# Query tensor of the first two batches spread over 128 partitions, score products in four row tiles, and a new order for the opening of a memory-attention and feed-forward kernel

## Chip, core and metric

The kernel runs on one core of a Trainium2 chip. The metric is the device time of one execution in microseconds (us). Before the change three runs took 653.88, 654.03 and 655.69 us, so the median is 654.03 us.

## What is computed

For each of 8 batches and 8 heads there are 576 positions, a head size of 64 and 32 memory slots. A softmax over the positions turns `phi` into weights, these gather `k` and `v` into 32 slots, and the queries attend to the slots. The result goes through a two-layer feed-forward stage.

```python
a = softmax(phi, axis=2)                        # over the 576 positions
k_m = einsum('bhsm,bhsd->bhmd', a, k)
v_m = einsum('bhsm,bhsd->bhmd', a, v)
attn = softmax(q @ k_m.T / sqrt(64), axis=-1)   # over the 32 slots
x = (attn @ v_m)  ->  (4608, 512)
h = x @ w_in                                    # 512 x 2048, 64-bit floats in memory
out = maximum(0.01 * h, h) @ w_out              # 2048 x 512, 64-bit floats in memory
```

## The kernel before

**Staging.** The slot values `v_m` are multiplied into `w_in` ahead of time (the "fold", `fold_products`, L1003), so that the first layer is a product of the attention weights with a folded weight, and the second layer a product with `w_out`. The 4608 rows are worked through in groups. Group 0 (384 rows of batch 0) is computed in f32 straight from the weights, since the split of the weights into pairs of f16 words is not there yet; all later groups use three f16 products for one. The opening is the part from the first instruction to the end of group 0. In it the first two batches' attention, the loading of the weights and their conversion from 64-bit floats, and group 0 itself run beside each other.

**Names.** Each step has a name in a dictionary, and two strings of names, `OPENING` (L47) and `LATER` (L67), give the order in which the steps are written. Each engine takes its instructions in exactly that order. The steps that the change and the prediction speak of:

- `a0.phi0`, `a0.k`, `a0.q0`, `a0.v`: loads of batch 0, issued on SyncE's queue (SP). `i0.ld0` to `i0.ld2` load the first quarter of `w_in` in three pieces (768, 768 and 512 columns), `o0.ld0` to `o0.ld2` that of `w_out`. A staging tile of eight slots (`ld_slot`) takes q and the pieces in turn.
- `a0.A10`, `a0.A11` (L592): maxima of phi on DVE. `a0.A2` (L633) transposes them on PE, `a0.A3` (L640, L643) reduces them and writes a diagonal matrix, `a0.B0` (L649) spreads them to all partitions with a product of ones by that diagonal. `B1x` subtracts (L658), `B2x` is the exponential on ACT (L664), `B3` sums (L680 to L683).
- `a0.C10`, `a0.C11` (L698): 72 small products each that gather k and v into slots. `C2` (L712) transposes the sums, `C30` (L721 to L726) turns them into factors, `C3k` (L743, ACT) scales the slots of k and lays them out three times side by side, `C31` (L754, DVE) scales those of v into `x_v`. `C4` (L762, L337, L339) and `D2` (L344) find the largest slot value.
- `D10` (L777): four PE transposes of the scaled k into 96 partitions, `D3` (L799) copies them to `kT`. `Q0`, `Q1` (L845): DVE transposes of q in blocks of 32. `E10`, `E1` (L887): score products, 24 each for batch 0, in three row tiles of 32 by four column tiles of 32. `E20` to `E22` (L908): DVE transposes of the scores.
- `S01` to `S06`: the softmax of the first two thirds of batch 0 (maximum L928, subtract L931, exponential L936, sum L940 to L942, scale L945, transpose L953). `S11` to `S18`: the last third.
- `D11` (L785) and `D5` (L805): the transpose of `x_v` into `vT`. `f00.1` (L1020): the first fold, eight products of 64 by 32 by 512. `f00.2` (L1370): its copy into `w_mem`. `f01`, `f02`, `f03` are the other quarters.
- `i0.y0` (L397, ACT), `i0.h0` (L386 on ACT or L388 on DVE), `i0.t0` (L406, DVE): the two halves of a 64-bit word are scaled or shifted and put together as one f32 word, for piece 0 of the first quarter of `w_in`; `i0.b` (L411) sums squares.
- `u0.P0` (L1114): the first product of group 0, two f32 products of 128 x 384. `u0.V0` (L1121) is its activation, `u0.O0` (L1186) three f32 products of 128 x 512 with `w_out`. There are 16 of each.
- `z.1`, `z.3`, `z.4` (L1387): that many products of a tile of ones, whose result nobody reads.

A product of f32 operands appears in the trace as two MATMUL records.

q of batches 0 and 1 is loaded to 96 partitions, six positions to a partition:

```python
t = (ld_slot() if b < FB else at(IO * g, IO))[:CP].rearrange(
    "p (hh j d) -> p hh j d", hh=HP, j=NJ
)
nc.sync.dma_start(
    t, q[b].rearrange("(hh g) (p j) d -> g p hh j d", g=NG, j=NJ)[g]
)
```

k, v and phi are already loaded to 128 partitions, nine positions to a partition.

Of the kernel before, what the change touches and what calls it, by code (L numbers as in the profile page):

```python
# [40 lines left out]
a0.C10 i0.ld0 i0.ld1 a0.B3 a0.C2 i0.ld2 z.1 a0.C30 a0.v a0.C3k a0.D10 a0.Q0 a0.D3 a0.E10 a0.Q1
a0.E1 i0.y0 i0.h0 o0.ld0 i0.t0 z.3 a0.E21 a0.E20 i0.y1 i0.h1 o0.ld2 a0.S01 o0.ld1 o1.ld0 i0.y2
i0.h2 i0.t2 a0.C11 a0.S02 i0.t1 a0.S03 i0.b a0.E22 a0.S11 a0.C31 o0.y0 a0.D11 a0.S12 a0.D5 f00.1
o0.h0 a0.S04 i1.ld1 o0.y2 a0.S05 f00.2 a0.S06 a0.C4 z.1 a0.S13 u0.P0 a0.D2 o0.t0 a0.S14 a0.S15
a0.D4 i1.ld0 o0.h1 u0.V0 o0.y1 u1.P0 u1.P1 o0.h2 u1.V0 o0.t2 i1.ld2 a0.S16 o1.ld2 o1.y0 o1.h0 u0.O0
# [5 lines left out]
i2.b u4.V0 a1.B20 u5.P0 a1.B3 o0.b a1.C10 i3.ld2 a1.Q0 i3.ld1 a1.C2 u5.V0 o1.b u2.O1 i3.y0 u5.P1
u4.V1 a1.C30 a1.C31 a1.C3k a1.C4 a1.D10 a1.D2 o2.b i3.h0 a1.D3 a1.Q1 i3.y2 i3.h2 a1.D11 a1.D4 u3.O1
i3.t2 a1.E1 o3.ld0 a1.D5 i3.y1 u4.O0 i3.h1 i3.t0 o3.h0 u5.V1 o3.y0 o3.ld2 u5.O0 a1.E20 i3.t1 a1.E21
i3.b ci.1 o3.ld1 a1.E22 f03.1 a1.S01 a1.S11 a1.S02 a1.S03 a1.S04 u4.O1 o3.y2 o3.y1 o3.h2 ci.2 o3.t0
f03.2 a1.S12 ci.3 ci.4 e. o3.h1 o3.t1 a1.S05 u6.P0 u6.V0 a1.S13 a1.S06 a1.S07 u6.P1 u7.P0 a1.S14
a1.S15 o3.t2 w0.2 u7.V0 u6.O0 a1.S16 o3.b w1.1 co.1 co.2 u7.O0 w1.2 co.3 u6.V1 co.4 u5.O1 o0.k0
# [1423 lines left out]
```

## Time and profile before

| | |
|---|---|
| median of three runs (lowest, highest) | 654.03 us (653.88, 655.69) |
| profiled execution: from its first to its last instruction (span) | 653.4 us |
| what lies around that span (lowest run less the span) | 0.5 us |
| PE busy | 635.2 us, 97% of the span |
| DVE busy | 515.4 us, 79% |
| ACT busy | 392.5 us, 60% |
| mean granted PE clock | 0.995 |
| moved by DMA | 61.16 MB |

For the profiled execution the profile gives no other time than its span. The page of the profile gives busy times of an engine, then digits for 40 equal slices of the span (16.3 us each), then groups of instructions. An engine's timeline lists instructions in order of time: start, duration, engine, line, operation, output and input, count, and in brackets the idle time ahead of it with what ended it. A row of the view by stretches gives, for each stretch, the busy time and number of instructions of PE, weight loads, DVE, ACT and GpSimd, then the granted PE clock, the busy share of the DMA engines and the GB/s that they moved.

### The profile page before, as it was taken

The numbers are of one execution on the slowest core, as the hardware profiler recorded it, in microseconds if no ns is written. First come the engines' busy times: TensorE is split into PE (matmuls) and PEld (weight loads), VectorE is DVE, ScalarE is ACT, GpSimd is POOL, SyncE is SP. The second block draws the span as 40 slices with busy tenths as digits, with TensorE's granted clock in tenths as the row PEclk, the third lists the DMA queues.
The fourth block names the chain that finished last, engine by engine and source line by source line (L and its number), as shares of the span: only waits on it lengthen the run. The fifth ranks groups of instructions, "written<-read, shape, count | busy, mean of one in ns | idle before, by whom it ended". The sixth has DMA issues, their size and how long they took to land.

```text
span 653.4 us, 17090 instructions
## 1 busy us (share of the span) xinstructions
PE 635.2 (97%) x7256; PEld 476.3 (73%) x7256; DVE 515.4 (79%) x863; ACT 392.5 (60%) x671; POOL 29.5 (5%) x37
## 2 busy tenths in 40 slices
PE   6799999999999999999999999999999999999997
...
PEclk9799999999999999999999999999999999999999
DMA  9999722105601753431155011064104110010102
GB/s 237 405 340 332 246 89 85 46 7 104 194 3 25 142 155 56 111 124 35 25 117 158 1 33 43 11 134 146 34 15 80 27 29 22 14 29 6 34 1 50
DMA packets 85309, 61.16 MB, mean 94 GB/s; under 512 B 61936, under 2 KB 68336, under 8 KB 85232
## 3 DMA queue, kind: packets, MB, share of 16 engines
...
q10 hardware_dynamic: 96, 0.13, 0.1%
...
## 4 chain that ended last, share of the span: by engine, by line
PE 94%; DMA 2%; ACT 2%; SPq 1%; DVE 0%; issue 0%; ACTq 0%
PE po L1297 31%; PE ph L1229 22%; PE po L1186 16%; PE ph L1114 8%; PE ph L1297 5%; PE pa L1020 4%; PE pa L698 3%; DMA arena<-in_moe_w_in_dram 2%; PE po L1331 1%; PE pa L861 1%; PE pa L1387 1%; ACT wi L1245 1%; PE pa L887 0%; PE pa L344 0%; SPq L549 0%
## 5 line engine op out<-in xcount | busy, mean ns | idle before, releaser
L1297 PEld LDWEIGHTS <-arena 128*128 128x128 f16 x2184 | 209.9, 98 | 31.9 <-issue 8.8
L1245 ACT ACTIVATE wi<-ph,g_sc 128x256 f32<-128x256 f32 (+1 forms) x224 | 99.3, 466 | 164.4 <-PE ph L1229 156.9
L1229 PE MATMUL ph<-a,w_mem 128*128 128x256 f16 (+3 forms) x1440 | 145.3, 246 | 2.9 <-ACT wi L1245 2.9
L1229 PEld LDWEIGHTS <-w_mem 128*128 128x128 f16 x1440 | 114.6, 98 | 17.9 <-issue 6.3
L1297 PE MATMUL po<-arena 128*128 128x256 f16 x936 | 122.2, 273 | 0.0
L1297 PE MATMUL po<-wo,arena 128*128 128x256 f16 x936 | 122.1, 273 | 0.0
L1186 PE MATMUL po<-wo,arena 128*128 128x512 f16 (+1 forms) x384 | 110.3, 433 | 0.0
L1274 DVE TENSOR_TENSOR arena<-arena 128x1024 f16<-128x1024 f32 x52 | 63.6, 1223 | 22.4 <-ACT arena L1270 22.4
L1274 DVE TENSOR_TENSOR arena<-wi,arena 128x768 f16<-128x768 f32 (+1 forms) x60 | 54.7, 912 | 10.1 <-ACT arena L1270 10.1
L1266 DVE TENSOR_TENSOR arena<-wi 128x256 f32<-128x256 f32 x104 | 40.4, 430 | 25.6 <-ACT wi L1245 25.1
L1270 ACT CAST arena<-arena 128x1024 f16<-128x1024 f32 x52 | 54.5, 1047 | 8.2 <-DVE arena L1266 8.0
L1114 PE MATMUL ph<-a,w_mem 128*128 128x192 f16 (+2 forms) x304 | 52.2, 317 | 0.7 <-ACT t L936 0.7
L1186 PEld LDWEIGHTS <-arena 128*128 128x128 f16 x288 | 27.9, 98 | 29.7 <-issue 0.6
L1270 ACT CAST arena<-wi 128x768 f16<-128x768 f32 (+1 forms) x60 | 46.6, 777 | 1.5
L1266 DVE TENSOR_TENSOR arena<-wi,arena 128x256 f32<-128x256 f32 x104 | 45.8, 440 | 1.8
L1297 PE MATMUL ph<-wo,arena 128*128 128x256 f16 x312 | 42.6, 273 | 0.0
L985 POOL TENSOR_TENSOR a<-t,a 128x1024 f16<-128x1024 f32 (+2 forms) x16 | 21.9, 1385 | 431.9 <-ACT a L980 431.9
L1186 PEld LDWEIGHTS po<-wo,arena 128*128 128x128 f32 x96 | 17.7, 190 | 20.3 <-issue 18.5
L1020 PE MATMUL pa<-wi,vT 64*32 64x512 f16 (+1 forms) x704 | 28.9, 420 | 0.4 <-ACT vT L805 0.4
L1114 PEld LDWEIGHTS <-w_mem 128*128 128x128 f16 x240 | 20.7, 98 | 10.3 <-issue 4.1
L1053 ACT ACTIVATE w_mem<-pa 128x512 f16<-128x512 f32 x40 | 22.7, 596 | 8.4 <-PE pa L1020 7.4
L1121 ACT ACTIVATE arena<-ph,g_sc 128x384 f32<-128x384 f32 x32 | 18.4, 581 | 15.6 <-PE ph L1114 15.3
...
## 6 DMA issues: line engine op xcount, KB each, us to landing
...
arena<-in_k_dram SPq DMA_DIRECT2D x28, 288.0 KB, 4.7
arena<-in_v_dram SPq DMA_DIRECT2D x28, 288.0 KB, 4.9
...
```

Source lines behind the costliest of these rows:

```text
L698: nc.tensor.matmul(var["pk"][g][hh * M:(hh + 1) * M, cs], ld["phi"][rows, hh, j, :], ld["kv", hh][rows, kinds[0]:kinds[-1] + 1, j, :], sta ...
L985: nc.gpsimd.tensor_tensor(piece(lo, tb), piece(t2, tb), piece(hi, tb), ALU.subtract)
L1020: nc.tensor.matmul(pf[g][cols, :], lhs, rhs, start=(n == 0), stop=(n == len(passes) - 1), tile_position=(g * D, hh * M),)
L1053: nc.scalar.activation(tiles(halves(w16(b, j), g)[:, 0]), w(g), AF.Copy, scale=ws)
L1114: nc.tensor.matmul(ph[:, t0:t0 + n * SB], lhs, rhs, start=(m == 0), stop=(m == len(seq) - 1))
L1186: nc.tensor.matmul(po, lhs, rhs, start=(f == 0 and m == 0), stop=(f == NQ * NF - 1 and m == len(seq) - 1),)
L1229: nc.tensor.matmul(ph[:, t0:t0 + n], lhs, rhs, start=(m == 0), stop=(m == len(seq) - 1))
L1245: nc.scalar.activation(dst, ph, AF.Prelu, scale=g_sc2[:, j:j + 1], alpha=SLOPE)
L1266: nc.vector.tensor_tensor(gt[:, x], y, z, op)
L1270: nc.scalar.copy(dst[:, 0], src)
L1274: nc.vector.tensor_tensor(dst[:, 1], src, dst[:, 0], ALU.subtract)
L1297: nc.tensor.matmul(acc, g[:, x, s, u], rhs, start=(h == 0 and j == 0 and u == 0 and m == 0), stop=(j == NQ - 1 and u == 1 and m == 2), ski ...
```

## The change

**q.** q of batches 0 and 1 now has the layout of k: 128 partitions with nine positions each, two heads in each of the two loads. The DVE transposes L845 become 128 x 1152 where they were 96 x 1536, and the rows of the output are written back in the matching order.

**Scores.** The slots of k are laid out twice in place of three times, two transposes (L788 of the new file) replace four, and `kT` is 128 x 256 where it was 96 x 512. For batch 0 the score products stand in four row tiles (16 of 288 columns in `E10`, for heads 0 and 1, and 16 in `E1`), and their results lie in two banks of the pool `ps_h`, one of `ps_o` and one of `ps_a` in place of three of `ps_a`. For batch 1 `E1` does three row tiles (24 products of 288 columns), and a new step `E3` does the fourth (8 of 192 columns, 8 of 96), and there is one `u` step between them. The DVE transposes of scores are cut in two parts: `E20` to `E23` and, for batch 0, `F20` to `F23`.

**Small steps.** `A3` and `C4` write no diagonal matrix any more; the products behind them take the maximum itself, repeated along the columns, as their stationary operand. One of four operations of `C30` is gone, its factor goes into the copy `D3`. The sum `B3` of batch 0 is cut in `B4` and `B3`. `C11` of batch 0 runs through the heads in its outer loop, through the nine positions in the inner one. `f0j.2` is cut in two steps, with four copies of 256 columns for two of 512.

**Products of ones.** `z.4`, `z.1`, `z.3`, `z.1` become `z.1`, then a new step `y.` of 35 products of 32 x 32 by 8 columns, `z.1`, `z.2` and `z.2`.

**Order.** `OPENING` is a new list. `LATER` is the same list.

```diff
-    CP = 96
-    NJ = S // CP
-    NB = CP // 32
+    NB = 3
+    BJ = KJ // NB
+    NR = P // 32
...
-            t = (ld_slot() if b < FB else at(IO * g, IO))[:CP].rearrange(
-                "p (hh j d) -> p hh j d", hh=HP, j=NJ
-            )
+            t = ld_slot()[:, 0:2 * KJ * D].rearrange("p (hh j d) -> p hh j d", hh=2, j=KJ)
             nc.sync.dma_start(
-                t, q[b].rearrange("(hh g) (p j) d -> g p hh j d", g=NG, j=NJ)[g]
+                t,
+                q[b].rearrange("h s d -> (h s) d").rearrange(
+                    "(hh gp j) d -> gp hh j d", gp=P, j=KJ
+                )[:, 2 * g:2 * g + 2],
             )
...
-                var["diag"] = diag = att.tile([P, NG, P], F32, name="r1k", bufs=2)
-                for g in range(NG):
-                    nc.vector.tensor_scalar_mul(diag[:, g, :], ident, mx2[:, g:g + 1])
+                var["mx2"] = mx2
...
-                        pb[g * D:(g + 1) * D].rearrange("p hh m -> p (hh m)"), ones[:, :D],
-                        var["diag"][:, g], start=True, stop=True, tile_position=(0, g * D),
+                        pb[g * D:(g + 1) * D].rearrange("p hh m -> p (hh m)"),
+                        var["mx2"][:, g:g + 1].broadcast_to([P, D]), ident,
+                        start=True, stop=True, tile_position=(0, g * D),
...
-            for j in range(KJ):
-                for hh in range(HP):
+            inner = b == 0 and kinds == (1,)
+            for j, hh in (
+                [(j, hh) for hh in range(HP) for j in range(KJ)] if inner
+                else [(j, hh) for j in range(KJ) for hh in range(HP)]
+            ):
...
-            var["pkT"] = pkT = ps_a.tile([CP, NG, ND, P], F32, name="pa")
-            for g in range(NG):
-                for db in range(ND):
-                    nc.tensor.transpose(
-                        pkT[:, g, db, :],
-                        var["x_k"][:, g, db].rearrange("p tb x -> p (tb x)"), ident,
-                    )
+            var["pkT"] = pkT = ps_a.tile([P, ND, P], F32, name="pa")
+            for db in range(ND):
+                nc.tensor.transpose(
+                    pkT[:, db, :], var["x_k"][:, db].rearrange("p g h x -> p (g h x)"), ident,
+                )
...
+            for j0, j1 in js:
                 for db in range(ND):
-                    for hh in range(HP):
-                        for tb in range(NB):
-                            rows = slice(tb * 32, (tb + 1) * 32)
-                            cols = slice(hh * M, (hh + 1) * M)
+                    for hh in heads:
+                        for r in rs:
+                            rows, cols = slice(r * 32, (r + 1) * 32), slice(hh * M, (hh + 1) * M)
+                            t, x = bank_of(r, j0)
                             nc.tensor.matmul(
-                                psc[tb][cols, g, :], var["kT"][rows, g, db, cols],
-                                var["qT", g][rows, hh, :, db, :],
+                                var["psc"][t][cols, x:x + (j1 - j0) * 32],
+                                var["kT"][rows, db, cols],
+                                var["qT", hh // 2][rows, hh % 2, j0:j1, db, :],
...
+    def short_products(n):
+
+        pi = ps_a.tile([P, NF, P], F32, name="pa")
+        for x in range(n):
+            r, c = 0, x % 4 * 32
+            nc.tensor.matmul(
+                pi[c:c + 32, 0, 0:8], ones[r:r + 32, 0:32], ones[r:r + 32, 0:8], start=True,
+                stop=True, tile_position=(r, c),
+            )
+
+    steps["y."] = lambda: short_products(SHORT)
...
-a0.phi0 a0.A10 z.4 a0.phi1 a0.A11 a0.A2 a0.k a0.A3 a0.B0 a0.q0 a0.B10 a0.B11 a0.B20 a0.q1 a0.B21
+a0.phi0 a0.A10 z.1 y. a0.phi1 a0.A11 a0.q0 z.1 a0.A2 a0.A3 a0.k a0.B0 a0.B10 a0.B20 a0.q1 i0.ld0 z.2
```

**Three places in the order.** First SyncE's queue, from the last load of k to the first of `w_out`, before the change (wi_89 and wo_92 to wo_94 hold k and then v, arena is the staging tile):

```order
L549 DMA wi_89<-in_k_dram 128x576
L583 DMA arena<-in_q_dram 96x4x384 x2
L376 DMA arena<-in_moe_w_in_dram 128x512
L376 DMA arena<-in_moe_w_in_dram 128x256 x2
L376 DMA arena<-in_moe_w_in_dram 128x512 x2
L549 DMA wo_92<-in_v_dram 128x576
L549 DMA wo_93<-in_v_dram 128x576
L549 DMA wo_94<-in_v_dram 128x576
L549 DMA wi_89<-in_v_dram 128x576
L372 DMA arena<-in_moe_w_out_dram 128x768
```

The same queue after the change, from the first load of q, which stands right behind phi:

```order
L583 DMA arena<-in_q_dram 128x2x576
L551 DMA wo_92<-in_k_dram 128x576
L551 DMA wo_93<-in_k_dram 128x576
L551 DMA wo_94<-in_k_dram 128x576
L551 DMA wi_89<-in_k_dram 128x576
L583 DMA arena<-in_q_dram 128x2x576
L378 DMA arena<-in_moe_w_in_dram 128x512
L378 DMA arena<-in_moe_w_in_dram 128x256 x2
L378 DMA arena<-in_moe_w_in_dram 128x512 x2
L374 DMA arena<-in_moe_w_out_dram 128x512
L551 DMA wo_92<-in_v_dram 128x576
```

Half of q moved ahead of k, and a piece of `w_out` of 512 columns moved ahead of v.

Second DVE, before the change, from the last transpose of scores of batch 0 to the end of `S06` (t_308 holds scores, x_v the scaled slots of v, a the finished attention weights):

```order
L908 STREAM_TRANSPOSE t_308<-pa 128x384
L928 TENSOR_REDUCE tm<-t_308 128x12
L754 TENSOR_SCALAR x_v<-po,r_228 128x64 x2
L940 TENSOR_REDUCE ts__420<-t_308 128x24
L941 TENSOR_SCALAR ts__420<-ts__420 128x24
L942 RECIPROCAL ts__420<-ts__420 128x24
L945 TENSOR_TENSOR t_308<-t_308,ts__420 128x768
L953 STREAM_TRANSPOSE a<-t_308 128x768
```

DVE after the change, from the subtraction `S02` to the end of `S06` (t_317 holds scores, wi_86 is the first quarter of `w_in`):

```order
L971 TENSOR_TENSOR t_317<-t_317,tm 128x768
L939 STREAM_TRANSPOSE t_317<-pa 128x96
L408 SCALAR_TENSOR_TENSOR wi_86<-arena 128x768
L408 SCALAR_TENSOR_TENSOR wi_86<-arena 128x512
L766 TENSOR_SCALAR x_v<-po,r_261 128x64 x2
L408 SCALAR_TENSOR_TENSOR wi_86<-arena 128x768
L980 TENSOR_REDUCE ts__420<-t_317 128x24
L981 TENSOR_SCALAR ts__420<-ts__420 128x24
L982 RECIPROCAL ts__420<-ts__420 128x24
L939 STREAM_TRANSPOSE t_317<-ph 128x96
L985 TENSOR_TENSOR t_317<-t_317,ts__420 128x768
L993 STREAM_TRANSPOSE a<-t_317 128x768
```

The step `C31` (x_v) now has a piece of `w_in` (`i0.t1`) and a transpose of scores (`F20`) behind it, ahead of the end of `S06`.

Third PE, before the change, from the end of `C11` to the second fold (wi_86 and wi_87 are the first two quarters of `w_in`):

```order
L698 MATMUL po<-wo_94,wi_88 32x64 x2
L698 MATMUL po<-wi_89,wi_88 32x64 x2
L785 MATMUL pa<-ident,x_v 128x128
L1020 MATMUL pa<-wi_86,vT 32x512 x8
L1387 MATMUL pa<-ones 128x512
L1114 MATMUL ph<-a,w_mem 128x384 x2
L344 MATMUL pa<-mdiag,ones 128x128
L1114 MATMUL ph<-a,w_mem 128x384 x4
L1186 MATMUL po<-wo_91,arena 128x512 x3
L1114 MATMUL ph<-a,w_mem 128x384 x2
L1186 MATMUL po<-wo_91,arena 128x512 x6
L1020 MATMUL pa<-wi_87,vT 32x512 x8
```

PE after the change, from `C11` to the second fold:

```order
L712 MATMUL po<-wo_92,wi_88 32x64 x18
L712 MATMUL po<-wo_93,wi_88 32x64 x18
L712 MATMUL po<-wo_94,wi_88 32x64 x18
L712 MATMUL po<-wi_89,wi_88 32x64 x18
L795 MATMUL pa<-ident,x_v 128x128
L1060 MATMUL pa<-wi_86,vT 32x512 x8
L1154 MATMUL ph<-a,w_mem 128x384 x4
L346 MATMUL pa<-ident,m_464 128x128
L1227 MATMUL po<-wo_91,arena 128x512 x3
L1154 MATMUL ph<-a,w_mem 128x384 x4
L1227 MATMUL po<-wo_91,arena 128x512 x3
L1060 MATMUL pa<-wi_87,vT 32x512 x8
```

`C11` goes head by head, the product of ones ahead of `u0.P0` is gone, and the second fold stands ahead of `u0.O1`, behind six products of `w_out` where nine stood.

More of the change, by code (lines that the diff above doesn't have):

```diff
@@ L39 @@
 OPENING = """
-a0.phi0 a0.A10 z.4 a0.phi1 a0.A11 a0.A2 a0.k a0.A3 a0.B0 a0.q0 a0.B10 a0.B11 a0.B20 a0.q1 a0.B21
[L41 to L45, printed above, removed]
@@ L51 @@
[L51 to L56, printed above, removed]
@@ L57 @@
-a1.S08 o0.k1 o0.k2 u7.P1 e2. o0.l0 u7.V1 o0.l1 u6.O1 a1.S17 a1.S18 o0.l2 u7.O1
+a0.phi0 a0.A10 z.1 y. a0.phi1 a0.A11 a0.q0 z.1 a0.A2 a0.A3 a0.k a0.B0 a0.B10 a0.B20 a0.q1 i0.ld0 z.2
+a0.B11 a0.B21 a0.C10 a0.B4 a0.B3 a0.C2 i0.ld1 a0.C30 i0.ld2 o0.ld2 a0.v a0.C3k a0.Q0 a0.D10 a0.D3
+a0.Q1 a0.E10 a0.E1 a0.F21 i0.y0 i0.y2 a0.E21 z.2 a0.F22 a0.E23 i0.h0 a0.E22 a0.E20 i0.y1 o0.ld0
+i0.h1 a0.S01 a0.S02 a0.C11 a0.F23 i0.h2 i0.t0 o0.y2 a0.S03 i0.t2 a0.C31 i0.t1 a0.D11 a0.S04 a0.D5
+i1.ld1 a0.F20 f00.1 o0.y0 o0.h0 f00.3 f00.2 a0.S05 a0.S06 a0.S11 o0.t0 o1.ld0 a0.S12 u0.P0 i0.b
@@ new lines @@
+a1.B0 i1.b a1.B10 o2.t2 u3.V0 f02.3 a1.B20 u5.P0 u3.O0 u4.P0 u5.V0 a1.B3 a1.C10 i2.b a1.q1 a1.Q1
+a1.C2 a1.C30 u5.P1 i3.ld2 i3.ld1 u2.O1 a1.C31 a1.C4 i3.y0 a1.D2 a1.D11 u4.V0 o3.ld0 o1.b a1.C3k
+u4.V1 a1.D10 o0.b i3.h0 u3.O1 i3.t0 i3.y2 a1.D3 a1.D4 a1.D5 i3.h2 a1.Q0 o3.ld1 a1.E1 u4.O0 a1.E21
+a1.E20 i3.y1 o2.b i3.h1 a1.E22 a1.E3 u5.O0 i3.t1 a1.E23 i3.t2 o3.y0 o3.h0 u5.V1 o3.ld2 a1.S01 i3.b
+a1.S11 f03.1 a1.S02 ci.1 o3.h2 a1.S03 ci.2 u4.O1 o3.y1 o3.y2 f03.2 a1.S04 o3.h1 o3.t0 ci.3 o3.t2
+u6.P0 f03.3 ci.4 u6.V0 a1.S12 e. a1.S13 a1.S05 o3.t1 u7.P0 u6.P1 a1.S14 a1.S06 a1.S15 w1.1 w0.2
@@ new lines @@
+o3.s0 a2.q1 o3.k1 o3.k0 o3.l1 P16.0 P16.1 o3.k2 O13.0 V16.0 C15 o2.m3 o3.s1 O13.1 V16.1 C16 o3.l0
+o3.s2 o3.m1 a2.C2 a2.C30 i0.l1 o3.l2 o3.m2 P17.0 L15 o3.m3 o3.n3 O14.0 V17.0 L16 a3.phi P17.1 a2.Q0
+a2.C3k V17.1 C17 O14.1 o3.n1 a2.D10 i0.l0 a2.Q1 a2.D3 P18.0 O15.0 V18.0 a2.C31 o3.n2 i0.l2 O15.1
+o3.m0 P18.1 a2.E1 a2.E22 a2.E3 a3.kv3 i1.k0 L17 a2.E21 a2.E23 V18.1 i1.l0 P19.0 a2.E20 a2.C4 i1.k1
+Z1.2 a3.kv2 P19.1 a2.D11 a2.S01 C18 Z1.1 a3.kv1 Z1.0 a2.S02 L18 V19.0 O16.0 i1.k2 a2.D2 a2.D4 a3.kv0
@@ L683, in _ @@
             nc.vector.tensor_tensor(s0, s0, ph[:, :, 8], ALU.add)
+        @step("B3")
+        def _():
+            if b == 0:
+                return sums_of(4)
+            var["s0"] = s0 = att.tile([P, HP, M], F32, name="r1k", bufs=2)
+            nc.vector.tensor_reduce(
+                s0, ld["phi"].rearrange("p hh j m -> p hh m j"), AX.X, ALU.add
+            )
+        if b == 0:
+            steps[f"{name}B4"] = lambda: sums_of(0)
         def slots_of(kinds):
```

383 lines of the change are left out of this document (201 added, 182 removed).

## Prediction

> **What bounds the kernel now.** I read the page first: which engine is full, and in which slices of the span.
>
> ```profile
> PE 635.2 (97%) x7256; PEld 476.3 (73%) x7256; DVE 515.4 (79%) x863; ACT 392.5 (60%) x671; POOL 29.5 (5%) x37
> ...
> PE   6799999999999999999999999999999999999997
> ...
> PEclk9799999999999999999999999999999999999999
> DMA  9999722105601753431155011064104110010102
> ```
>
> PE is full from the third slice on; only the first two (32 us) have room. The clock dips and DMA is full there too. So the time is the moment at which the unbroken work of PE begins, plus that work. PE's timeline gives the moment: `u0.P0`, L1114, at 32.68.
>
> ```profile
> 0.99 6.05 PE L1387 MATMUL pa<-ones 128*128 128x512 f32 x8 [0.99 <-POOL ones L269]
> 6.88 0.27 PE L633 MATMUL pa<-ident,r1k 128*128 128x128 f32 x1
> ...
> 19.05 1.41 PE L887 MATMUL pa<-wo,kT 32*32 32x192 f32 x39 [1.06 <-issue]
> 22.19 4.84 PE L1387 MATMUL pa<-ones 128*128 128x512 f32 x6 [1.73 <-DVE t L908]
> ...
> 29.86 1.09 PE L1020 MATMUL pa<-wi,vT 64*32 64x512 f32 x16 [0.36 <-ACT vT L805]
> ...
> 32.68 1.53 PE L1114 MATMUL ph<-a,w_mem 128*128 128x384 f32 x4 [0.67 <-ACT t L936]
> ...
> 36.85 2.74 PE L1186 MATMUL po<-wo,arena 128*128 128x512 f32 x6
> ```
>
> The useless `z.3` takes 4.84 us ahead of `C11`. Six such records of useful work take 2.74, so the clock was at half. The chain that ended last has `C11` next:
>
> ```profile
> 27.03 1.63 PE po L698 x102
> ```
>
> Then DVE's timeline leads to `u0.P0`; its last row ends at 32.53.
>
> ```profile
> 28.64 0.48 DVE L754 TENSOR_SCALAR x_v<-po,r 128x64 f32<-128x64 f32 x2 [1.34 <-PE po L698]
> 29.03 0.94 DVE L940 TENSOR_REDUCE ts__420<-t 128x24 f32<-128x768 f32 x1
> ...
> 31.55 0.98 DVE L953 STREAM_TRANSPOSE a<-t 128x768 f32<-128x768 f32 x1
> ```
>
> So `C11` at 27.0 holds DVE, and DVE holds `u0.P0`. `C11` needs v. The last v load is issued at 16.69 (SyncE's timeline) and takes 8.4 us (the row of the DMA issues, last number): 25.1. From there on `z.3` holds it. The loads of q stand in the same rows.
>
> ```profile
> 3.69 1.28 SPq L583 DMA_DIRECT2D arena<-in_q_dram  x2
> ...
> 16.69 0.33 SPq L549 DMA_DIRECT2D wi<-in_v_dram  x1
> ...
> 50.34 0.37 SPq L583 DMA_DIRECT2D arena<-in_q_dram  x1
> ```
> ```profile
> wi<-in_v_dram SPq DMA_DIRECT2D x1, 288.0 KB, 8.4
> ```
>
> Why v lands so late is in the view by stretches (last number: GB/s):
>
> ```profile
> 8.00:15.00 7.00, 3.98 (x155) 2.54 (x155) 5.12 (x12) 1.99 (x4) 0.00 (x0) 1.00 1.08 213
> 16.00:22.00 6.00, 2.96 (x96) 1.43 (x90) 2.72 (x3) 2.76 (x4) 0.00 (x0) 0.78 1.05 399
> ...
> 51.00:52.00 1.00, 1.00 (x5) 0.52 (x3) 0.76 (x2) 0.90 (x2) 0.00 (x0) 1.00 1.08 390
> 56.00:57.00 1.00, 1.00 (x4) 0.49 (x3) 1.00 (x1) 1.00 (x4) 0.00 (x0) 1.00 1.05 241
> ```
>
> From 8 to 15 us, while q (1.18 MB) is on its way, DMA is 108% busy and moves 213 GB/s; afterwards 399. The same recurs when q of batch 1, issued at 50.34, moves: 241, against 390 shortly before. The load to 96 partitions goes at about half the pace of the others.
>
> **The change part by part.** *q on 128 partitions.* From 8 to 15 us 7 x 213 = 1.49 MB moved; at 399 GB/s that is 3.7 us, so everything behind q lands 3.3 us earlier. The bounds: 0 if the pace stays 213 (a rival), 3.4 if all of it reaches 406. Ahead of v now stands a piece of `w_out` of 512 KB (0.52 MB): 1.3 us back. v is complete at 25.1 - 3.3 + 1.3 = 23.1.
>
> *`C11` head by head.* The heads land one after another, so only the last head's 18 products remain. Below: a quarter of 1.63, 0.4. Above: 18 records of 64 columns in a row on one tile, at 2.74/6 = 0.46 us for 512 columns, 1.0. Sums in one tile follow each other, so I take 0.95. `C11` ends at 24.1 in place of 28.66.
>
> *Behind `C11`.* `C31` now stands in DVE's queue ahead of `i0.t1` and `F20`, with `S04` to `S06` behind all of them. Their prices:
>
> ```profile
> 21.56 1.04 DVE L908 STREAM_TRANSPOSE t<-pa 128x384 f32<-128x384 f32 x2
> ...
> 25.27 0.95 DVE L406 SCALAR_TENSOR_TENSOR wi<-arena 128x768 uint32<-128x768 uint32 x1
> ```
>
> Before, `C31` starts at 28.64, the next instruction 0.39 later, and from 29.03 to 32.53 `S04` to `S06` take 3.5. After: 24.1 + 0.39 + 0.95 (`t1`) + 0.25 (`F20`, a quarter of a transpose of 0.52 and its start) + 3.5 = 29.2, and `u0.P0` 0.15 later, as before: 29.35. That is 3.3 us earlier. The fold beside it: `f00.1` starts when `t1` ends, 25.45; its copy, two of 0.53 (31.10), is now four of 0.3 to 0.5:
>
> ```profile
> 18.96 0.92 ACT L397 ACTIVATE arena<-arena 128x768 f32<-128x768 f32 x1 [3.15 <-DMA arena<-in_moe_w_in_dram]
> 31.10 1.05 ACT L1370 COPY w_mem<-pa 128x512 f32<-128x512 f32 x2
> ```
>
> Before, it started 1.24 after `f00.1`; now at 26.7 to 27.0 (two conversions of 0.92 stand ahead of it on ACT), so it ends at 28.0 to 29.0: hidden under DVE by 0.2 to 1.2.
>
> *The scores' chain* must reach `C31` by 24.1. Two of its steps gain for sure:
>
> ```profile
> 3.58 2.18 DVE L592 TENSOR_REDUCE r1k<-wi 128x64 f32<-128x576 f32 x2 [3.58 <-DMA wi<-in_phi_dram]
> ...
> 7.61 0.48 DVE L643 TENSOR_SCALAR r1k<-ident,mx 128x128 f32<-128x128 f32 x2
> ...
> 13.80 1.77 DVE L845 STREAM_TRANSPOSE wi<-arena 96x1536 f32<-96x1536 f32 x1
> ```
>
> The maxima are ready at 5.76, but `A2` waited for `z.4` until 6.88. Two `z.1` take 4 x 6.05/8 = 3.0 us; the 35 tiny products are 70 records, at 11 ns (1.63 us for `C11`'s 144) to 36 ns (`E1`, 1.41/39) 0.8 to 2.5 us: done at 4.8 to 6.5, so 0.4 to 1.1 won. Two diagonal steps (0.48) go, the transposes of q become three quarters as long (0.44 each), `D10` and `C30` shrink by 0.5. Against that q0 (0.59 MB) stands ahead of k: up to 1.6 us later at 0.37 MB/us, an estimate between 213 and 399. So `E1`, which ended at 20.46, ends between 16.5 and 18.9. Six transposes (1.6), maximum and subtraction (0.95 each), `F23` (0.25), `t0` and `t2` (0.95 and 0.64) make 5.3: DVE reaches `C31` at 21.8 to 24.2. v decides, with 2.3 us to spare or none.
>
> *PE's work behind `u0.P0`.* Batch 1's part of it:
>
> ```profile
> 60.10 0.44 PE L649 MATMUL pa<-r1k,ones 128*64 128x128 f32 x4
> ...
> 72.03 0.60 PE L777 MATMUL pa<-ident,x_k 128*96 128x128 f32 x4
> ...
> 75.47 1.93 PE L887 MATMUL pa<-arena,kT 32*32 32x192 f32 x96
> ```
>
> `D10` loses two of four: -0.3. Scores: three row tiles hold 9216 x 3/4 columns, 1.93 x 0.75 = 1.4; the fourth, `E3`, works on four column tiles only: below a quarter of 1.93, 0.5; above, if they overlap, 2 x (192 + 96) columns of two records each, 1152 x 0.46/512 = 1.0. I take 1.0: +0.5, with `D10` +0.2. That column tiles of one row group overlap is seen in L649: four records on two of them take 0.44, four transposes one after another 0.60.
>
> *`f01.1` ahead of `u0.O1`.* It comes 2.6 us earlier counted from `u0.P0`. Its weights were done here:
>
> ```profile
> 42.27 1.55 DVE L406 SCALAR_TENSOR_TENSOR wi<-arena 128x768 uint32<-128x768 uint32 x2
> ```
>
> that is at 43.8, while `f01.1` ran at 45.96: 2.1 to spare, 2.6 wanted; the loads are 3.3 earlier as is PE. 0 to 0.5, I take 0.4.
>
> *At nothing:* the operations saved in `C30` and `C4` of later batches (PE is full beside them; if DVE were the bound, a gain of 0.5 a batch), the repeated maximum as stationary operand (same shapes), the output rows (same sizes), two more ACT copies per fold (0.2; ACT is idle 40%), the banks in `ps_h` (released by `F20`, ahead of `S06`).
>
> **Sum**, against the profiled execution: 653.4 - 3.3 + 0.2 + 0.4 = 650.7 us of span. The runs' median is 0.6 above that span, so 651.3.
>
> **The rivals.** *A: v is not what DVE waits for.* If v lands at 21.5 (a faster start of DMA), the scores' chain decides: `C31` at 22.5, `u0.P0` 5.25 later at 27.75, 4.9 won: 649.7. For it: DMA had slow rows only with q. Against: the w_out piece ahead of v. 14%.
>
> *B: the clock is at half when PE's unbroken work begins.* It has been before:
>
> ```profile
> 19.00:20.00 1.00, 0.95 (x39) 0.71 (x38) 0.00 (x0) 1.00 (x2) 0.00 (x0) 0.71 1.03 393
> 20.00:21.00 1.00, 0.46 (x9) 0.00 (x0) 0.32 (x1) 0.72 (x2) 0.00 (x0) 0.50 1.04 389
> ...
> 26.00:27.00 1.00, 1.00 (x8) 0.14 (x10) 0.96 (x3) 0.98 (x2) 0.00 (x0) 0.88 1.02 418
> ```
>
> It fell at about 19.4 after small products and idling, and rose at about 26.2, 4.1 us after `z.3` began. After the change `z.2` ends near 20, then come only small products, and no `z` ahead of `u0.P0`. Price: the last head of `C11` 0.95 longer, and 4.1 us at half speed, 2.05 lost: 651.3 + 3.0 = 654.3 at most, 653.6 if it rises earlier. Against: from 8 to 15 us PE was busy 4.0 of 7 us, nearly all with small products, and the clock stayed at 1.00. 17%. [...]
>
> *C: `E3`'s column tiles do not overlap.* Then its 32 records of 144 columns on average run one by one, 0.13 each: 4.1 in place of 1.0, so 654.4. Against it stands L649. 6%. [...]
>
> *D, slower: q does not get faster.* If 213 GB/s belongs to q's source and not to its 96 partitions, v lands at 25.1 + 1.3 = 26.4. PE then stands idle from 20 to 26, since `z.3` is gone, and the half clock of B comes with it. The change is (landing - 23.1) - 2.7 + 3.0: slower from a landing at 22.8 with half clock, by over 0.3% from 24.8; at 26.4 it gives 657.6. Against: phi, k and v of batch 1, in the layout that q gets, moved at 390 (51 to 52 us). 8%.
>
> **How the numbers follow.** The forecast has 55%, its own range 650.3 to 652.2. 0.3% is about what a measurement of this kernel can tell: 2.0 us, so faster means below 652.1. From the forecast 50, from A 14, from B 2: faster 0.66. Same: 5 + 15 + 6 + 1: 0.27. Slower: D, 0.07. The range 649.2 to 654.4 leaves out D and the ends of A and B, some 15%.
>
> **What would show it.** Right: GB/s near 390 between 8 and 12 us; the last v landing near 23; `C11` ending 1 us later; `C31` ending DVE's wait for PE; `u0.P0` at 29 to 30; clock 1.00 from there. Wrong: PE idle or at half clock behind `u0.P0`; a wait of PE ahead of `f01.1` of over 1 us; `E3` over 2 us; rows near 213 GB/s ahead of 15 us.

## The result, and the profile after

The changed kernel takes 661.12 us (median of 4 runs, 660.74 to 661.92) against 653.95 us (4 runs, 653.69 to 655.69): a ratio of 1.0106, 95% interval 1.0089 to 1.0124. It is slower by 7.2 us, where 651.3 was forecast. The page of the profile hardly shows it; PE is still full from the third slice on, and its clock dips in the second and the third:

```profile
span 659.2 us, 17106 instructions
...
PE 638.9 (97%) x7268; PEld 478.2 (73%) x7268; DVE 510.2 (77%) x851; ACT 390.7 (59%) x679; POOL 29.4 (4%) x37
...
PEclk9789999999999999999999999999999999999999
```

PE's timeline does. The rows from 2.99 to 46 are the opening; 78 and 82 are batch 1's scores; the product at 222.09 waits 0.56 for ACT in every kernel of this study and serves as a mark; the last two rows are far behind the opening.

```profile
2.99 1.14 PE L1442 MATMUL pa<-ones 32*32 32x8 f32 x70
...
12.19 0.33 PE L712 MATMUL po<-wo,wi 64*32 64x64 f32 x7
16.42 0.24 PE L712 MATMUL po<-wo,wi 64*32 64x64 f32 x1 [3.90 <-issue]
...
23.00 2.50 PE L1430 MATMUL pa<-ones 128*128 128x512 f32 x4
25.44 2.67 PE L712 MATMUL po<-wo,wi 64*32 64x64 f32 x102
...
28.08 1.00 PE L712 MATMUL po<-wi,wi 64*32 64x64 f32 x30
...
34.02 4.51 PE L1154 MATMUL ph<-a,w_mem 128*128 128x384 f32 x8 [2.43 <-DVE a L993]
...
46.42 1.09 PE L1060 MATMUL pa<-wi,vT 64*32 64x512 f32 x16
...
78.29 1.47 PE L906 MATMUL pa<-arena,kT 32*32 32x288 f32 x48
...
82.46 1.18 PE L906 MATMUL pa<-arena,kT 32*32 32x192 f32 x32
...
222.09 0.81 PE L1270 MATMUL ph<-a,w_mem 128*128 128x256 f16 x6 [0.56 <-ACT wi L1286]
...
256.69 0.60 PE L1270 MATMUL ph<-a,w_mem 128*128 128x256 f16 x4 [0.39 <-issue]
...
502.49 0.38 PE L1338 MATMUL ph<-wo,arena 128*128 128x256 f16 x2 [0.91 <-issue]
```

Five records before the end of `C10` PE stands still for 3.90 us, and the profile shows no wait for another engine or a transfer ("issue"). The kernel before has such a row too, 1.06 in the middle of the scores (19.05). In both traces the stop comes after exactly 222 weight loads and 221 or 222 products. What is behind it: the sums of the exponentials are ready at 11.41, but DVE gets the transpose of them only at 17.02; the scores follow at half clock; `C11` begins at 25.44 and takes 3.64 us to 29.08, where it took 1.63; and `u0.P0` starts at 34.02, its first eight records at half clock (4.51 us; the next eight such records, at 41.17, take 2.74). DVE's rows:

```profile
11.12 0.29 DVE L684 TENSOR_TENSOR r1k<-r1k,wi 128x128 f32<-128x128 f32 x1
...
17.02 0.29 DVE L734 TENSOR_REDUCE r<-po 128x2 f32<-128x128 f32 x1 [5.61 <-PE po L726]
...
29.12 0.48 DVE L766 TENSOR_SCALAR x_v<-po,r 128x64 f32<-128x64 f32 x2 [0.92 <-PE po L712]
...
32.90 0.98 DVE L993 STREAM_TRANSPOSE a<-t 128x768 f32<-128x768 f32 x1
```

By stretches (clock third from the end, GB/s last), DMA does what was forecast, and the clock does not:

```profile
8.00:12.00 4.00, 4.00 (x115) 1.89 (x117) 3.02 (x7) 1.25 (x2) 0.00 (x0) 1.00 1.04 380
12.00:16.00 4.00, 0.52 (x50) 0.36 (x36) 0.00 (x0) 0.00 (x0) 0.00 (x0) 1.00 1.03 403
...
17.00:24.00 7.00, 5.04 (x67) 2.26 (x68) 4.08 (x10) 5.41 (x10) 0.00 (x0) 0.52 1.04 404
...
34.00:38.00 4.00, 3.98 (x7) 2.16 (x8) 2.48 (x7) 2.83 (x6) 1.88 (x3) 0.57 0.49 192
```

The 1.00 of the first row holds from 10.4 us on, where the records of the clock begin; ahead of that, from 7.62, four useless products take 3.36 us, which take 1.98 in the runs below at full clock.

SyncE's timeline and the row of the DMA issues give v:

```profile
14.20 1.15 SPq L551 DMA_DIRECT2D wi<-in_v_dram  x1
```
```profile
wi<-in_v_dram SPq DMA_DIRECT2D x1, 288.0 KB, 7.9
```

Its last load is issued at 14.20 and takes 7.9: it lands at 22.1, ahead of the forecast 23.1.

**One more profile of the kernel before** (the ninth run below) changes the yardstick. Its span is 651.4 us in a run of 653.30, near the median, and in it `u0.P0` starts at 29.62, not at 32.68. Against that profile the changed kernel is 7.8 us longer in three parts: 34.02 - 29.62 = 4.40 up to `u0.P0`; 1.69 from there to the mark (222.09 - 34.02 against 216.00 - 29.62); 1.71 behind the mark, of which the two late stops are 0.39 + 0.91 = 1.30. Of the 1.69 about 1.0 is the clock: eight records lose 1.77 in the changed kernel (4.51 for 2.74), and four lose 0.79 in that profile of before (2.24, where such four take 1.45 further on). What the rest of it is, no run shows.

### The profile page after: what moved, and what is told of

It is laid out like the page before. It is cut to its first block, busy times and chain, and to the rows that moved or that the text cites. A ratio compares the mean times of both kernels' runs of the same rounds, so it can differ in the third digit from the quotient of the medians.

```text
span 659.2 us, 17106 instructions
## 1 busy us (share of the span) xinstructions
PE 638.9 (97%) x7268; PEld 478.2 (73%) x7268; DVE 510.2 (77%) x851; ACT 390.7 (59%) x679; POOL 29.4 (4%) x37
## 4 chain that ended last, share of the span: by engine, by line
PE 96%; issue 1%; ACT 1%; DVE 1%; POOL 0%; ACTq 0%; POOLq 0%
PE po L1338 31%; PE ph L1270 22%; PE po L1227 16%; PE ph L1154 8%; PE ph L1338 5%; PE pa L1060 4%; PE pa L712 3%; PE pa L1430 1%; PE po L1372 1%; PE pa L870 1%; PE po L712 1%; ACT wi L1286 1%; PE ph L906 0%; PE pa L906 0%; PE pa L346 0%
## 5 line engine op out<-in xcount | busy, mean ns | idle before, releaser
L1154 PE MATMUL ph<-a,w_mem 128*128 128x192 f16 (+2 forms) x304 | 53.7, 323 | 2.4 <-DVE a L993 2.4
L1227 PEld LDWEIGHTS <-arena 128*128 128x128 f16 x288 | 27.8, 98 | 29.7 <-issue 0.6
L1227 PEld LDWEIGHTS po<-wo,arena 128*128 128x128 f32 x96 | 17.5, 190 | 21.1 <-issue 17.9
L1161 ACT ACTIVATE arena<-ph,g_sc 128x384 f32<-128x384 f32 x32 | 18.3, 580 | 16.5 <-PE ph L1154 16.3
L1093 ACT ACTIVATE w_mem<-pa 128x512 f16<-128x512 f32 x40 | 22.7, 595 | 8.5 <-PE pa L1060 7.4
```

The lines of the kernel that those rows point to most:

```text
L1093: nc.scalar.activation(tiles(halves(w16(b, j), g)[:, 0]), w(g), AF.Copy, scale=ws)
L1154: nc.tensor.matmul(ph[:, t0:t0 + n * SB], lhs, rhs, start=(m == 0), stop=(m == len(seq) - 1))
L1227: nc.tensor.matmul(po, lhs, rhs, start=(f == 0 and m == 0), stop=(f == NQ * NF - 1 and m == len(seq) - 1),)
```

## The experiments

The theory: PE is supplied with instructions in pieces, the tiny products use up what it holds, and it stops in `C10` until the next piece has come. The page has a queue `q8 instruction` with 57 packets, 0.93 MB; taken as PE's, for 7268 products and 7268 loads, that is some 250 of them to a packet (255, or 247 if the 444 ahead of the first stop were there before), an estimate. 222 of each are 444, somewhat under two packets; that waits which leave no row make up the rest is assumed, not shown. Rivals: `C10`'s data, and the clock. All runs in one table (us; "first stop" is PE's idle time, put down to `issue`, behind the first 221 or 222 products, and the 0.15 is too short for the timeline to mark it; the eight records are those of `u0.P0` and `u1.P0`, 2.74 at full clock; ratios are against runs of the kernel before beside them, with the 95% interval):

| kernel | first stop | u0.P0 | 8 records | mark | span | time | ratio |
|---|---|---|---|---|---|---|---|
| before, first profile | 1.06 | 32.68 | | 218.01 | 653.4 | 653.95 | |
| before, again | 0.15 | 29.62 | | 216.00 | 651.4 | 653.58 | 1.0008 (0.9989 to 1.0027) |
| changed | 3.90 | 34.02 | 4.51 | 222.09 | 659.2 | 661.12 | 1.0106 (1.0089 to 1.0124) |
| 1: no tiny products | 0.28 | 29.26 | 4.22 | 217.78 | 653.3 | 655.12 | 1.0019 (1.0003 to 1.0036) |
| 2: before, with tiny products | 4.91 | 34.98 | | 221.21 | 656.6 | 659.91 | 1.0099 (1.0067 to 1.0132) |
| 3: old order of C11 | 3.25 | 32.32 | 5.46 | 221.37 | 659.0 | 660.97 | 1.0108 (1.0080 to 1.0136) |
| 4: products ahead of u0.P0 | 4.08 | 33.82 | 2.82 | 220.77 | 659.4 | 660.93 | 1.0104 (1.0076 to 1.0132) |
| 5: DMA quiet near 11 us | 0.69 | 38.10 | 2.82 | 224.60 | 662.5 | 664.2 (one run) | |
| 6: as 1 and 4 together | 0.30 | 29.43 | 2.82 | 215.55 | 651.3 | 653.57 | 0.9997 (0.9983 to 1.0012) |
| 7: 17 tiny products | 1.31 | 32.44 | 5.43 | 220.98 | 658.4 | 657.63 | 1.0074 (1.0048 to 1.0099) |
| 8: as 1 and 3 together | 0.27 | 28.35 | 5.46 | 217.07 | 652.5 | 653.89 | 1.0016 (1.0001 to 1.0030) |
| 10: as 1, 3 and 4 together | none | 28.93 | 2.82 | 215.11 | 650.8 | 653.03 | 0.9998 (0.9989 to 1.0007) |
| 11: 29 tiny products | 0.59 | 32.34 | 4.51 | 220.71 | 656.1 | 657.48 | 1.0042 (1.0028 to 1.0056) |

**1. The changed kernel without the tiny products**

```
-a0.phi0 a0.A10 z.1 y. a0.phi1
+a0.phi0 a0.A10 z.1 z.1 a0.phi1
```

> The changed kernel with the 35 tiny products replaced by one product of 512 columns: 4 PE records and loads in place of 140, PE busy for about the same time. Theory (supply): in both traces PE stops for instructions behind 222 weight loads, for 1.06 us in the scores before and for 3.90 us at the end of C10 after; the tiny products use up 70 of the 222. Without them the stop has to move 68 loads further on, out of C10 into the scores, C10 ends near 12.6 in place of 16.7, the scores end near 18 to 19 in place of 23.1, v (22.1) decides, and u0.P0 starts 4 to 5 us earlier, near 29 to 30: 655 to 657. First rival (data): the stop belongs to C10's operands or its release, not to the count; then it stays at 12.5 to 16.4 and the time at 661. Second rival (clock): the tiny products only mattered for the clock; then no stop moves and the time changes by under 1.5 us.

The stop moved into the scores and shrank. PE's timeline of this kernel:

```profile
17.17 0.42 PE L906 MATMUL ph<-wo,kT 32*32 32x288 f32 x1 [0.28 <-issue]
...
19.73 2.83 PE L712 MATMUL po<-wo,wi 64*32 64x64 f32 x108
23.12 1.20 PE L712 MATMUL po<-wi,wi 64*32 64x64 f32 x36 [0.56 <-DMA wi<-in_v_dram]
24.88 0.33 PE L795 MATMUL pa<-ident,x_v 128*128 128x128 f32 x1 [0.56 <-DVE x_v L766]
...
29.26 4.22 PE L1154 MATMUL ph<-a,w_mem 128*128 128x384 f32 x8 [2.43 <-DVE a L993]
```

`u0.P0` at 29.26 is what the prediction said for the changed kernel (29.35), and the time falls by 6.0 us, as the theory had it. The data rival is out: `C10`'s operands are the same. So is the clock rival, by which no stop would have moved and the time would have changed by under 1.5. The record at which it stops is again the one behind 221 products.

**2. The kernel before, with the 35 tiny products in place of two of its useless ones**

```
-a0.phi0 a0.A10 z.4 a0.phi1
+a0.phi0 a0.A10 z.1 y. z.1 a0.phi1
```

> The kernel before, with the first two batches as they were, and only the opening products changed: one product of 512 columns, the 35 tiny ones, one more of 512 columns, in place of four of 512. Theory (supply): the 222nd weight load now falls on C10's last records, so PE stops there and not in the scores, and starts again only when the next instructions have come, which was at 19.05; the scores move back by 3 to 5 us and the time is 2 to 4 us longer than before, 656 to 658. Rival (data): PE reaches A2 0.7 us earlier and nothing stops: 654, or up to 0.7 less.

```profile
16.99 0.37 PE L698 MATMUL po<-wi,wi 64*32 64x64 f32 x2 [4.91 <-issue]
```

The stop sits two records before the end of `C10`, behind 221 products, and 5.7 us are lost: 35 products of 8 columns, which take 1.14 us themselves, cost the old kernel most of what the whole change costs. The mark moves by 5.2 against the second profile of before. The place is as the theory had it, the size is not: it had 2 to 4 us, and a stop until 19.05 where PE goes on at 16.99.

**3. The changed kernel with `C11` in the old order**

```
-            inner = b == 0 and kinds == (1,)
+            inner = False
```

> The changed kernel with C11 in the old order, slot by slot over the heads. Theory: head by head the 18 products of a head follow each other on one column tile, and C11 takes 3.6 us where it took 1.6; in the old order it takes 1.6 to 1.9, u0.P0 comes 1.7 to 2.0 us earlier, 659.2. Rival: C11 is long because the heads of v land one after another (the last only near 28); then it keeps its 3.6 us and the time stays at 661.

```profile
32.32 5.46 PE L1154 MATMUL ph<-a,w_mem 128*128 128x384 f32 x8 [2.43 <-DVE a L993]
```

`C11` shrinks from 3.64 to 1.7 us and `u0.P0` comes 1.70 earlier, as expected; the time, for which 659.2 was expected, does not change. (`C11` ends 2.35 earlier. Of that 0.36 is an earlier start, and 0.64 is lost again, since the product behind it waits 1.20 for DVE and not 0.56.) The clock takes 0.95 of it back (5.46 for 4.51), so that the mark is 0.72 earlier; the stops at 256 and 502 (0.83 and 0.59 in this trace) add 0.12, and the runs of the two kernels spread over more than is left. What the prediction said of v (only its last head remains) holds only where `C11` waits for v at all; in the changed kernel v had landed 3.3 us before `C11` began.

**4. Two products of 512 columns between `f00.1` and `u0.P0`**

```
-a0.S12 u0.P0 i0.b
+a0.S12 z.2 u0.P0 i0.b
```

> The changed kernel with two products of 512 columns put into PE's queue between f00.1 and u0.P0, where PE stands idle from 31.6 to 34.0. Theory (clock): the granted clock falls to half at 34.3 to 37.7 because of that idle stretch, which costs 1.7 us; filled, the clock stays at 1.00, and the time is 1.2 to 1.7 us shorter, 659.5. Rival: the fall belongs to the sparse work further ahead (16 to 25); then it stays, and the time is 661 or longer by what the products delay u0.P0.

```profile
31.32 1.99 PE L1430 MATMUL pa<-ones 128*128 128x512 f32 x4
33.82 2.82 PE L1154 MATMUL ph<-a,w_mem 128*128 128x384 f32 x8 [0.51 <-DVE a L993]
...
255.41 0.39 PE L1338 MATMUL po<-wo,arena 128*128 128x256 f16 x2 [0.86 <-issue]
...
502.25 0.83 PE L1338 MATMUL ph<-wo,arena 128*128 128x256 f16 x6 [1.20 <-issue]
```

The clock stays up and the mark is 1.32 us earlier: the idle stretch is what let the clock fall here. It does not always do so: in run 5 PE stands idle for the same 2.43 us ahead of `u0.P0`, and the eight records take 2.82. The time misses the expectation all the same, because the late stops grew from 1.30 to 2.06 and a product at 340 waits 0.71 more.

**5. DMA quiet near 11 us, ahead of PE's stop**

```
-a0.B20 a0.q1 i0.ld0 z.2 a0.B11 a0.B21 a0.C10 a0.B4 a0.B3 a0.C2 i0.ld1
+a0.B20 a0.q1 z.2 a0.B11 a0.B21 a0.C10 a0.B4 a0.B3 a0.hold a0.C2 i0.ld0 i0.ld1
...
+            steps[f"{name}hold"] = lambda: nc.sync.dma_start(
+                dram.tile([P, 2], F32, name="d_hold"), var["s0"][:, 0, 0:2]
+            )
```

> The changed kernel with SyncE's queue held behind q1 until the sums of the exponentials are done (a transfer of 1 KB that reads them stands ahead of the weight loads and of v), so that no data moves for some us around 11 to 14. It is slower in time, since v and all weights come later; what counts is PE's stop at the end of C10. Theory (the refill of instructions queues behind data): in the changed kernel the refill starts 3.0 us after PE has passed the middle of what it held, with DMA 103% busy; where DMA is idle later in the span it starts within about 1 us. So here it starts near 12 to 12.5 in place of 14.0, and PE's stop is 1.5 to 2.5 us in place of 3.9. Rival (the refill takes that long by itself, or starts only when PE has nothing left): the stop stays at 3.5 to 4.

PE's timeline, and the stretches (DMA share second from the end):

```profile
13.80 0.24 PE L715 MATMUL po<-wo,wi 64*32 64x64 f32 x1 [0.69 <-issue]
...
38.10 2.82 PE L1157 MATMUL ph<-a,w_mem 128*128 128x384 f32 x8 [2.43 <-DVE a L996]
```
```profile
10.00:11.00 1.00, 1.00 (x2) 0.00 (x0) 0.90 (x4) 0.00 (x0) 0.00 (x0) 1.00 0.75 277
11.00:12.00 1.00, 1.00 (x61) 0.82 (x65) 0.27 (x1) 0.00 (x0) 0.00 (x0) 1.00 0.08 30
12.00:13.00 1.00, 1.00 (x102) 0.94 (x88) 0.00 (x0) 0.00 (x0) 0.00 (x0) 1.00 0.08 1
```

The stop stays at the same record, five before the end of `C10`, and shrinks from 3.90 to 0.69, more than expected. In the trace the first packet of the instruction queue runs from 10.88 to 12.35, in the changed kernel from 14.01 to 14.99. PE goes on 2.62 earlier (13.80 for 16.42); the other 0.59 is that it gets to the stop later (13.11 for 12.52). When the packet starts, PE has 83 products behind it here and all 222 in the changed kernel, so PE's place is not what the refill waits for. It starts as the loads run out, with DMA 75% busy from 10 to 11 and 8% from 11 to 13, where the changed kernel keeps it 103 to 104% busy. So the refill is held up by the loads of q and the weights. In all traces PE goes on 1.2 to 1.5 us after that packet has ended (16.42 after 14.99; 13.80 after 12.35). The middle of what PE held, in the expectation, is an estimate of the author's: half of the 444 records ahead of the stop, passed at 11.1 us in the changed kernel, 2.9 ahead of the packet's start at 14.01. Counted on by 255 records a packet, the 31 later packets that start there with DMA idle do so at most 0.64 behind their middle, 24 of them ahead of it; and in run 5 PE is short of the first one, so no run shows that a refill waits for it.

**6. Without tiny products, and with the two products ahead of `u0.P0`** (edits 1 and 4)

> The changed kernel without the tiny products (one product of 512 columns in their place) and with two products of 512 columns ahead of u0.P0. Without the tiny products alone u0.P0 starts at 29.26 but the clock falls to half from there on, 4.22 us for eight records that take 2.74 at full clock. Theory: filling PE's idle stretch of 2.43 us keeps the clock at 1.00, which brings 1.5 us: 653.6, and 652 to 652.9 if the stop of 0.7 us at 207 goes as well, as the count of instructions is 8 higher. Rival: late stops for instructions move elsewhere and eat the gain: 655.

```profile
26.92 1.98 PE L1430 MATMUL pa<-ones 128*128 128x512 f32 x4
29.43 2.82 PE L1154 MATMUL ph<-a,w_mem 128*128 128x384 f32 x8 [0.52 <-DVE a L993]
```

653.57 us, the theory's first figure: the clock stays at 1.00, and the kernel is level with before. The stop at 207 us (0.70 in run 1) is gone too, and for that case the theory had 652 to 652.9; this part missed.

**7. 17 tiny products** (`SHORT = 17`)

> The changed kernel with 17 tiny products in place of 35. Theory (supply): the stop stays behind 222 weight loads, which is now 28 records into the first half of the scores and no longer in C10; it lasts 1 to 2 us there, C10 ends near 12.3, u0.P0 starts near 29.3 as without tiny products, and the time is 654.5 to 656.5. Rival (the stop belongs to C10 whatever the count, or to the time for which PE works on tiny products): it stays at C10's end or shrinks in proportion to 2 us, and the time is 658.

```profile
17.69 0.68 PE L906 MATMUL ph<-wi,kT 32*32 32x288 f32 x1 [1.31 <-issue]
19.98 3.78 PE L1430 MATMUL pa<-ones 128*128 128x512 f32 x4
```

Place and length of the stop are as the theory had them: behind 221 products, now 27 records into the scores. `u0.P0` is not, 32.44 for 29.3, nor is the time (654.5 to 656.5); the rival's 658 is near, though the stop did leave `C10`. I had left out what follows: behind the stop the clock is at half, the useless products take 3.78 in place of 1.98, `C11` begins at 23.70 and takes 3.8. The profiled run (span 658.4) is the longest of the four, with a stop of 1.7 at 327 us; the median of 657.63 is 3.5 below the changed kernel.

**8. Without tiny products, `C11` in the old order** (edits 1 and 3)

> The changed kernel without the tiny products and with C11 in the old order. Without the stop, v decides: the last head's 36 records start when its data lands, at 23.12, and take 1.20. Theory: in the old order all 144 records wait for the last head and take 1.6 to 1.7; C11 ends 0.4 to 0.5 later, u0.P0 at 29.7, 655.6. Rival: head by head is the slower order in any case, as its 108 records of three heads took 2.83; then u0.P0 is at 29.3 or earlier.

```profile
21.64 0.25 PE L712 MATMUL po<-wi,wi 64*32 64x64 f32 x2 [0.41 <-DMA wi<-in_v_dram]
...
23.98 0.33 PE L795 MATMUL pa<-ident,x_v 128*128 128x128 f32 x1 [0.60 <-DVE x_v L766]
...
28.35 5.46 PE L1154 MATMUL ph<-a,w_mem 128*128 128x384 f32 x8 [2.43 <-DVE a L993]
```

`u0.P0` is 0.91 earlier in the old order, the number of the rival, but the order is not the reason. In this trace the last head of v is there at 21.64, in run 1 at 23.12. From that moment `C11` takes 1.73 us here (to 23.37) and 1.20 in run 1 (to 24.32), and the product behind it (L795) starts 2.34 and 1.76 later. So where `C11` waits for v, head by head is shorter by 0.5, as the theory had it; runs 6 and 10 below agree (1.19 and 1.52). When v lands differs from one execution to the next, by profile from 21.6 to 23.3 with this queue. The times show no difference between the two orders: 1.0019 and 1.0016 of the kernel before.

**9. The kernel before, unchanged**

> The kernel before, unchanged, for a second profile of it. The prediction set its sum against one profiled execution with a span of 653.4 us and put 0.6 us around it. In all runs listed since, the time is 1.7 to 1.9 us above the span. Theory: that holds for the kernel before too, and the execution profiled first was 1.2 us longer than the median one; the span is now 651 to 653 with a time 1.8 above it, and the difference lies ahead of u0.P0. Rival: before has only 0.6 around its span, the changed kernel 1.7, and 1.1 us of its loss lies outside the span; then the time is 0.4 to 0.8 above the span.

PE's timeline, and a stretch to set beside the 213 GB/s of the prediction:

```profile
17.07 1.07 PE L887 MATMUL pa<-wo,kT 32*32 32x192 f32 x39
18.80 2.84 PE L1387 MATMUL pa<-ones 128*128 128x512 f32 x6 [0.66 <-DVE t L908]
22.66 0.25 PE L698 MATMUL po<-wi,wi 64*32 64x64 f32 x2 [0.42 <-DMA wi<-in_v_dram]
...
29.62 2.24 PE L1114 MATMUL ph<-a,w_mem 128*128 128x384 f32 x4
```
```profile
8.00:15.00 7.00, 3.61 (x155) 2.23 (x155) 5.65 (x12) 2.57 (x5) 0.00 (x0) 1.00 1.07 300
```

The theory holds: the time is 1.9 above the span here (653.30 and 651.4) and 1.6 to 2.0 in every run listed (1.9 to 2.0 for the kernel before and run 2, 1.6 to 1.8 for the others). By that surplus the execution behind the prediction's profile took an estimated 655.3, more than 1 us above the median. In the second profile DMA moves 300 GB/s from 8 to 15, v is there at 22.66, the stop in the scores is 0.15, the useless products run at full clock (2.84 for 4.84), and `u0.P0` starts 3.06 us earlier. Of that 2.01 is left at the mark (216.00 for 218.01): the clock is at half from 27.8 to 31.2, and the four records of `u0.P0` take 2.24 for 1.53.

**10. Without tiny products, products ahead of `u0.P0`, old order of `C11`** (edits 1, 3 and 4)

> The changed kernel without the tiny products, with two products of 512 columns ahead of u0.P0, and with C11 in the old order: the three edits that each gained ahead of u0.P0. Without tiny products u0.P0 starts at 28.35 in the old order of C11 and at 29.26 head by head. Theory: u0.P0 starts near 28.5 at a clock of 1.00, 0.9 us ahead of the kernel that differs only in C11's order, and the time is 0.6 to 0.9 below it, 0.1 to 0.2% below the kernel before. Rival: C11 ends earlier but the idle stretch ahead of u0.P0 is not filled any more or a late stop for instructions takes it; then the time is that of the kernel before within 0.1%.

The clock stays up and the mark, 215.11, is the earliest of all; yet 653.03 us against 653.24 for the kernel before beside it is no difference that can be measured. The rival's number came, though not by its mechanism: no late stop shows in the trace. Against the second profile of before it gains 0.69 up to `u0.P0` (28.93 for 29.62) and 0.89 up to the mark; before's own runs beside it lie between 651.85 and 655.57. `u0.P0` is 0.50 ahead of run 6 (28.93 for 29.43), but v was there 0.86 earlier (22.43 for 23.29), so `C11`'s order gained nothing. No version tried here beats the kernel before.

**11. 29 tiny products** (`SHORT = 29`), so that the count of PE records is that of before

> The changed kernel with 29 tiny products in place of 35, which makes its count of PE records that of the kernel before, 7256. The changed kernel (7268 records) and its variants with 7268 and 7272 stop for instructions at the same two late records, near 256 and 502 us, for 0.3 to 1.2 us each; the kernel before stops at neither. Theory (what is held is refilled in pieces of some 256 instructions, and PE stops where a piece falls wholly into a dense run of small products): with the count of before the pieces end where they end there, and both late stops are gone; the first stop falls on the first records of E10 and lasts 1 to 2.5 us, u0.P0 starts at 31.5 to 32.7, and the time is 2.5 to 4 us below the changed kernel, 657 to 658.5. Rival (the late stops belong to the changed code of E1 and E3, whatever the count): they stay.

All of PE's waits for instructions in this kernel:

```profile
PE ph L906 <- issue: 0.6, 1, 0.6
...
PE pa L712 <- issue: 0.5, 1, 0.5
```

Six tiny products fewer, and the stops at 256 and 502 us are gone; the 0.5 is at 147 us, where the second profile of before has 0.18. The first stop is shorter than expected (0.59 for 1 to 2.5); `u0.P0` and the time are as expected. The runs with 7268 or 7272 records all stop at the same two records, numbers 2505 and 5690 of PE; runs with other counts elsewhere (207 and 211 us in runs 1 and 2, 327 in run 7) or hardly. So the late stops go with the count, not with the changed code. The some 256 instructions to a piece are the estimate above (14536 / 57 = 255); that a piece has to fall into a dense run of small products is shown by no run. The count says where a stop can fall, not that it does: run 1 has 0.70 at 207 us, and run 8, with the same 7200 records, has none.

## Why the prediction was wrong, point by point

**The scores' chain is the step that failed.** The prediction had `E1` end between 16.5 and 18.9; it ended at 23.07. Its terms for `A2`, the diagonals and the transposes came out (`A2` at 6.16, though the two `z.1` took 4.15 for 3.0; sums at 11.41 against 12.57; in run 1, without the tiny products, `E1` ended at 17.84), though the range is not what they add up to, which is 17.5 to 19.8. The 35 tiny products, however, were costed at their own 0.8 to 2.5 us (1.14 measured) and as nothing else. Their 140 instructions move the point where PE stops from the scores to the end of `C10`, where 288 instructions pass in 1.6 us. Runs 1, 2 and 7 show the cause by count, run 5 the length by DMA. The sign was in the rows quoted: `[1.06 <-issue]` at 19.05 was shown and not asked about.

**q and v: right in the row, wrong against the yardstick.** 380 and 403 GB/s were measured for 399, v came at 22.1 for 23.1, and rival D fell. But 3.3 us were won against an execution with 213 GB/s. By the second profile the same sum is 7 x 300 = 2.1 MB, 5.2 us at 402, 1.8 won and 1.3 given back: 0.5, and v lands at 22.1 in place of 22.66. Run 2, with q as before, has v at 22.7. So 0.5 is nearer the real size of this term, and v's landing differs by more than that from one execution to the next (21.6 to 23.3).

**`C11`: its condition failed.** "Only the last head's 18 products remain" needs PE at `C11` before v; v was there first, and the order then costs 3.64 for 1.7. Where `C11` does wait for v, the last head takes 1.20 and 1.19 behind it (runs 1 and 6), for 0.95 forecast, and the old order 1.73 and 1.52 (runs 8 and 10): there the reason given holds. That 0.95 is near is luck. The last head's 18 products are 36 records, not 18, and at the prediction's rate (0.46 us for 512 columns, so 57 ns for 64) they would take 2.1; they take 25 to 33 ns each. That sums in one tile follow each other was its assumption; what was measured is 25 ns a record in a row on one tile, 11 over the tiles in turn.

**Rival B, given 17%, came in part.** The clock was at half from 17.3 to 24.1 behind the stop, and again from 34.3 to 37.7, 1.77 us on eight records. The second dip needs no stop: it came in run 1 too, behind PE's idle 2.43 us ahead of `u0.P0`, and went when they were filled (runs 4, 6 and 10). The argument against it, that small products had kept the clock at 1.00 before, took PE's busy share for what decides. The runs do not show what does: run 5 has the idle 2.43 us and no dip, and the second profile of before has a dip from 27.8 to 31.2 with no idle stretch of over 1.17 us in the 8 us ahead of it.

**Behind `C31`: right.** 0.39 + 0.95 + 0.25 + 3.5 + 0.15 = 5.24 was forecast from its start to `u0.P0`; it was 29.12 to 34.02, 4.90. So was the new `u0.P0` without the stop: 29.35 forecast, 29.26 in run 1.

**Batch 1: right.** 1.47 and 1.18 for 1.4 and 1.0; rival C (4.1 for `E3`) fell: the 32 records of `E3` on four column tiles of one row group took 1.18, so they overlapped. `f01.1` (46.42) waits for nothing, 0.4 too much.

**"At nothing": failed for the count of instructions.** 12 records more make 1.30 us of late stops (run 11).

**The sum against the median: failed.** 0.6 was put around the span, and it is 1.9 to 2.0 for the kernel before; the profiled execution was not a median one. So the 3.3 us were largely the bad luck of one profile, and the repaired change (run 10) ends level with before.
